# Windowed attention and a feed-forward layer on one core: loads placed a turn earlier, block weights joined by shift-or, largest element by a bfloat16 product, small products grouped

## The chip, the cores and the metric

The kernel runs on one NeuronCore of one Trainium2 chip. The core has five engines, each with its own instruction queue, which it works off in order: TensorE (in profiles PE, its weight loads PEld), VectorE (DVE), ScalarE (ACT), GpSimd (POOL) and SyncE (SP), which here issues transfers. Transfers run on 16 DMA engines. TensorE writes to PSUM, which has eight banks; everything else lives in SBUF. The metric is the device time of the program in microseconds; less is better.

## The reference

Two stages in float32, cut to what matters. The inputs `q`, `k`, `v` are 8 batches x 8 heads x 576 positions x 64; the weights arrive as float64, `w_in` 512 x 2048 and `w_out` 2048 x 512.

```python
scores = scale * np.matmul(q, k.transpose(0, 1, 3, 2))
bias = slopes[:, None, None] * (-np.abs(rel).astype(np.float32))[None, :, :]
mask = (rel >= 0) & (rel < window)               # window = 128
scores = np.where(mask, scores + bias[None], -1000000000.0)
attn = softmax(scores)                            # max, exp, sum, divide
x = matmul(attn, v)  ->  4608 tokens x 512
h = x @ w_in
g = np.where(h >= 1, h, np.where(h <= -1, 0.0, (h + 1) ** 2 / 4))
out = g @ w_out
```

A query sees only the 128 keys up to itself, so a block of 128 queries needs two blocks of keys.

## The kernel before

**Chunks, pairs, turns.** The 4608 tokens are worked in 12 chunks of 384, three blocks of 128. A chunk has eight heads, taken as four pairs; the pairs are numbered p = 0 to 47, four to a chunk, and heads m = 2p and 2p + 1. Chunks 0 and 1 (`LIGHT = 2`) do attention in float32, head by head. From chunk 2 on (p >= 8) attention is done in split float16: a float32 tensor becomes a high and a low half, and a product becomes three products of halves. What the list of steps does for one pair is called a turn here.

**A turn from p = 8 on.** `load_all` (L304, L305, then `load_v`, L376) issues three transfers on SyncE's queue: q, k and v of a later pair. `reach_of` takes the largest absolute values: for v on VectorE (L384), for q and k a sum of absolute values per row on ScalarE (L318). `split_qk` (L367, L368) makes the float16 halves of q and k, `split_v` (L424, L425) those of v. `scores_of_pair` multiplies q and k (L453) and `soften` makes the exponentials: bias and maximum on VectorE (L476), exp on ScalarE (L478). `weights_t` transposes the normalised weights on TensorE (L497), splits them on ScalarE and VectorE (L509, L510) and masks them on GpSimd (L512, L514) into the tile `lu`. `values_of_pair` multiplies `lu` with the halves of v (L557). Once a chunk, `level` (L326 to L335) and `scale_all` (L341 to L358) turn the largest values of the next chunk's four pairs into scales.

**Largest element over partitions.** A column of 128 largest values, one per partition, must become one number in every partition. GpSimd makes a diagonal matrix of the column (L152 in `spread`, L335 in `level`), TensorE multiplies it with a matrix of ones in float32 (L157 in `scale_of`, L341 in `scale_all`), and VectorE takes the maximum of each row. `scale_of` does so 19 times before 175 us, for the weights' blocks, for x of chunks 0 and 1, and for `w_out`; `scale_all` does so ten times, two columns at once.

**Weights.** The float64 weights come in 16 blocks, fetched by `fetch_weights` on ScalarE's queue (`w_in`: L186, `w_out`: L189), each into a tile of its own. `float32_of` makes float32 from the two 32-bit words: two ScalarE instructions in place (L176, L177), then on VectorE a left shift (L178) and an integer sum (L179). `convert_in` and `convert_out` call it, once a block each. All of it happens during chunk 0; the tiles are used for q and k afterwards, with five buffers of one pair each.

**Feed-forward.** For each chunk and each of 16 blocks, `layer1` makes 12 products of 384 columns (L585 to L587), ScalarE, VectorE and GpSimd make g and its halves (L592, L593, L594, L601, L602), and `layer2` makes nine products of 512 columns (L616 to L618), two blocks later. In chunk 0 `layer2` is in float32 (L613).

**What sets the order.** Attention's steps stand in one list, `segments`. While a chunk's feed-forward runs, 32 half-steps a chunk, the next chunk's attention segments are put in between, evenly. A planner then goes through all instructions in this order and puts each on its engine's queue by its own estimate of when it is ready; a later instruction that it takes to be ready may pass an earlier one. `behind(instructions, f)` adds, for what `f` issues, an edge of issue order behind the named instructions. `done_t[m]` names instructions of `weights_t(m)`: from chunk 2 on one of ScalarE, one of VectorE and one of GpSimd, and in the chunks before one of each as well.

The list for the pairs from 8 on, before the change:

```python
if new: segments.append([lambda p=p: reach_of(p + NPAIR)])
segments.append([lambda p=p: scores_of_pair(p, (0, 1))])
if new and g == NPAIR - 1: segments.append([lambda c=c: level(c + 1)])
segments.append([lambda p=p: scores_of_pair(p, (2,))])
segments.append([lambda p=p: split_v(p)])
if p > M1 // 2: segments.append([lambda p=p: values_of_pair(p - 1)])
if new and g == NPAIR - 1: segments.append([lambda c=c: scale_all(c + 1)])
segments.append([lambda p=p: weights_t(2 * p)])
segments.append([split_qk(p + 1)] + [load_all(p + 5)])
segments.append([lambda p=p: weights_t(2 * p + 1)])
```

Of the kernel before, what the change touches and what calls it, by code (L numbers as in the profile page):

```python
# [8 lines left out]
F32 = mybir.dt.float32  # L9
F16 = mybir.dt.float16  # L10
BF16 = mybir.dt.bfloat16
F32R = mybir.dt.float32r
I32 = mybir.dt.int32
U32 = mybir.dt.uint32
# [6 lines left out]
def windowed_attention_then_ffn(  # L21
# [26 lines left out]
    P = 128  # L48
# [56 lines left out]
    for m in range(H):  # L105
# [9 lines left out]
                    compare_op=ALU.is_ge, fill=NEG)  # L115

    sums = const.tile([P, 2, NQB, 2], F32, name="sums")
    G.memset(sums, 1.0e-9)
# [15 lines left out]

    ones = const.tile([P, P], F32, name="ones")
    G.memset(ones, 1.0)
    s_in = const.tile([P, NFC], F32, name="s_in")
# [11 lines left out]
    def spread(name, rows):  # L149

        diag[name] = ap1.tile([P, P], F32, name=f"d_{name}", tag="d", bufs=2)
        G.tensor_scalar(diag[name], ident, rows, None, ALU.mult)  # L152

    def scale_of(name, s, i):

        b = bank(f"m_{name}")[:, :P]
        T.matmul(b, ones, diag.pop(name), start=True, stop=True)  # L157
        top = column(f"top_{name}", "top")
        V.tensor_reduce(top, b, X, ALU.max)
        ti = top.bitcast(I32)  # L160
        V.tensor_scalar(ti, ti, 0x7F800000, None, ALU.bitwise_and)
        V.tensor_scalar(i, top, 2.0 ** -100, 1.0 / TOP, ALU.max, ALU.mult)
        V.reciprocal(s, i)
# [4 lines left out]

    def float32_of(w, name, out=None):

        low, high = w[..., 0], w[..., 1]
        f = stg.tile([P] + list(w.shape[1:-1]), F32, name=f"f_{name}", tag="stg")
        fi = f.bitcast(I32)


        S.activation(high.bitcast(F32), high.bitcast(F32), AF.Prelu, scale=2.0 ** -112, alpha=2.0 ** 32)  # L176
        S.activation(low, low.bitcast(U32), AF.Copy, scale=2.0 ** -29)  # L177
        V.tensor_scalar(fi, high, 3, None, ALU.logical_shift_left)  # L178
        V.tensor_tensor(fi if out is None else out.bitcast(I32), fi, low, ALU.add)  # L179
        return f  # L180

    raw = {}

    def fetch_weights(fc):
        w1 = rawp.tile([P, NCC, P, 2], I32, name=f"rawi{fc}", tag=f"rawi{fc % 3}")
        S.dma_start(w1, wi32[:, 2 * fc * P:2 * (fc + 1) * P].rearrange("(c p) (f w) -> p c f w", p=P, w=2))  # L186

        w2 = rawp.tile([P, DM, 2], I32, name=f"rawo{fc}", tag=f"rawo{fc % 3}")
        S.dma_start(w2, wo32[fc * P:(fc + 1) * P, :].rearrange("p (f w) -> p f w", w=2))  # L189
        raw[fc] = (w1, w2)  # L190

    wide = {}

    def convert_in(fc):
        f = wide[fc] = wp.tile([P, NCC, P], F32, name=f"f_i{fc}", tag="f_i", bufs=3)
        float32_of(raw[fc][0], f"i{fc}", out=f)
        rows = column(f"rows_i{fc}", "rows")
        V.tensor_reduce(rows, f.rearrange("p c f -> p (c f)"), X, ALU.max, apply_absolute_value=True)
        spread(f"i{fc}", rows)
# [8 lines left out]
    def split_in(fc):  # L208
        if fc > 1:
            fall_in(fc)  # L210
        f, s1 = wide.pop(fc), s_in[:, fc:fc + 1]
        t = wi[fc] = wp.tile([P, 2, NCC, P], F16, name=f"wi{fc}", tag=f"wi{fc}")
        S.activation(t[:, 0], f, AF.Copy, scale=s1)
        V.scalar_tensor_tensor(t[:, 1], f, s1, t[:, 0], ALU.mult, ALU.subtract)  # L214
# [4 lines left out]
    def convert_out(fc):  # L219
        wf[fc] = wp.tile([P, DM], F32, name=f"wf{fc}", tag=f"wf{fc}")  # L220
        float32_of(raw[fc][1], f"o{fc}", out=wf[fc])
        S.activation(junk, wf[fc], AF.Abs, accum_out=rows_o[:, fc:fc + 1])
# [58 lines left out]
    def load_qk(p):  # L281
# [9 lines left out]
        for j, r in enumerate(lo_rows):  # L291
            DMA.dma_start(kr[r, j, :n], k[g * P + j * D:g * P + (j + 1) * D, (c + 1) * CH - n:(c + 1) * CH])

    def load_all(p):

        c, g = divmod(p, NPAIR)
        n = CH + before(c) * P
        if c == LIGHT:
            t = wp.tile([P, 2 * CH + P], F32, name=f"qk_{p}", tag=f"wo{NPAIR + g}")
        else:  # L300
            tag = ("rawi0", "rawi1", "rawi2", "rawo0", "rawo1")[p % 5]
            t = rawp.tile([P, 2 * CH + P], F32, name=f"qk_{p}", tag=tag)
        pair[p] = dict(q=t[:, :CH], k=t[:, CH:CH + n])
# [16 lines left out]
    def level(c):  # L320
# [11 lines left out]
        V.tensor_reduce(top[:, 1:2], tops.pop(c)[:, :NPAIR], X, ALU.max)  # L332
        d = diag[c] = ap1.tile([P, 2, P], F32, name=f"d_{c}", tag="qr")
        for a in range(2):
            G.tensor_scalar(d[:, a], ident, top[:, a:a + 1], None, ALU.mult)  # L335
        tops[c, "i"] = iq

    def scale_all(c):

        b = bank(f"m_{c}")[:, :2 * P]  # L340
        T.matmul(b, ones, diag.pop(c).rearrange("p a w -> p (a w)"), start=True, stop=True)  # L341
        i_2[c], s_2[c] = column(f"i_2{c}", "i_2", 3, 2), column(f"s_2{c}", "s_2", 3, 2)
# [9 lines left out]
        V.tensor_scalar(z_of[c], fade, i_2[c][:, 0:1], None, ALU.mult)  # L352
        if "t" not in rels:
            rels["t"] = rawp.tile([P, NQB, 2 * P], F32, name="rels", tag="rawo2")
        rels[c] = rels["t"][:, c % 2], rels["t"][:, 2]
        V.tensor_scalar(rels[c][0], rel, s_2[c][:, 0:1], -1.0e38, ALU.mult, ALU.max)
# [278 lines left out]
    for m in range(M1):  # L635
# [11 lines left out]
        if odd:  # L647
            part["v"] = [[lambda p=p: load_v(p + 4)]] if p < NPAIR else []
            part["v"] += [[lambda x=x: load_all(x)] for x in {5: (8, 9), 6: (10,), 7: (11,)}.get(p, ())]
            part["v"] += [[lambda x=x: reach_of(x)] for x in {3: (4, 5), 4: (6, 7), 6: (8,), 7: (9,)}.get(p, ())]  # L650
# [12 lines left out]
    segments += [[lambda: load_all(p8 + 4)], [lambda: scale_all(LIGHT)], [lambda: split_qk(p8)]]  # L663
    for p in range(M1 // 2, NP):
        c, g = divmod(p, NPAIR)
        new = p + NPAIR < NP
        if new:
            segments.append([lambda p=p: reach_of(p + NPAIR)])
        segments.append([lambda p=p: scores_of_pair(p, (0, 1))])
        if new and g == NPAIR - 1:  # L670
            segments.append([lambda c=c: level(c + 1)])
        segments.append([lambda p=p: scores_of_pair(p, (2,))])
        segments.append([lambda p=p: split_v(p)])
        if p > M1 // 2:
            segments.append([lambda p=p: values_of_pair(p - 1)])
            if g == 0:
                ready.append(len(segments))
        if new and g == NPAIR - 1:
            segments.append([lambda c=c: scale_all(c + 1)])
        segments.append([lambda p=p: weights_t(2 * p)])  # L680
        segments.append(([lambda p=p: split_qk(p + 1)] if p + 1 < NP else []) + ([lambda p=p: load_all(p + 5)] if p + 5 < NP else []))
        segments.append([lambda p=p: weights_t(2 * p + 1)])
    segments.append([lambda: values_of_pair(NP - 1)])
# [127 lines left out]
```

## Time and profile before

| | |
|---|---|
| median of 3 runs | 1027.91 us (1027.88 to 1031.63) |
| profiled execution | 1030.51 us |
| its span, first to last instruction | 1028.3 us |
| TensorE busy | 975.1 us, 95% |
| VectorE, ScalarE, GpSimd busy | 742.2, 618.2, 374.7 us |
| mean granted TensorE clock | 0.979 |
| read from HBM, written | 49.28 MB, 9.44 MB |

Times in the profile are counted from the first instruction. A row of a group gives line, engine, operation, tiles written and read, shapes and count, then busy time and mean length of one, then the engine's idle time just before and what ended it. A row of the list of waits gives who waited for whom: total, times, longest. TensorE's instructions are pipelined and the ends of its matmuls are modelled, so what one costs is read from start to start. Some matmul records can be missing.

### The profile page before, as it was taken

How to read it: one execution, taken by the hardware profiler on the slowest of the kernel's cores; microseconds unless marked ns; L12 is line 12 of the kernel's file. 1: busy time of each engine (PE TensorE's matmuls, PEld its weight loads, DVE VectorE, ACT ScalarE, POOL GpSimd, SP SyncE). 2: the span in 40 equal slices, each digit the busy share in tenths (PEclk: the TensorE clock that was granted, in tenths of full speed). 3: DMA queues.
4: the chain of work that ended last, by engine and by line, in shares of the span. 5: the costliest groups of instructions: out<-in, count | busy, mean ns of one | idle time of the engine just before them, and what ended most of it. 6: DMA issues, size and time to landing. Idle time of an engine off the chain costs nothing.

```text
span 1028.3 us, 17951 instructions
## 1 busy us (share of the span) xinstructions
PE 975.1 (95%) x6218; PEld 548.8 (53%) x6218; DVE 742.2 (72%) x2128; ACT 618.2 (60%) x1547; POOL 374.7 (36%) x479
## 2 busy tenths in 40 slices
PE   7579999997899899899999999999999999999998
PEld 7446554554455455455555555555555555555554
DVE  5789889887767677777777777777777867775322
ACT  4678878665756655655755765765755755654332
POOL 5332211334344323433433433433434434334221
PEclk9889999999799999999999999999999999999999
DMA  8445442002101101201211201111101100000000
GB/s 258 159 154 168 160 142 85 1 11 73 52 22 57 57 24 35 69 30 39 68 40 40 74 24 47 57 30 57 60 29 57 50 2 1 32 1 1 32 1 31
DMA packets 53275, 59.88 MB, mean 58 GB/s; under 512 B 3520, under 2 KB 42432, under 8 KB 53184
## 3 DMA queue, kind: packets, MB, share of 16 engines
q1 hardware_dynamic: 42432, 41.96, 13.0%
q10 hardware_dynamic: 10752, 16.78, 4.8%
q8 instruction: 49, 0.80, 0.3%
q14 instruction: 42, 0.34, 0.1%
HBM read 49.28 MB, written 9.44 MB: 57 GB/s over the span
## 4 chain that ended last, share of the span: by engine, by line
PE 81%; DVE 8%; DMA 4%; ACT 3%; issue 2%; POOL 1%; ACTq 0%; SPq 0%; DVEq 0%; POOLq 0%
PE h L585 11%; PE h L587 11%; PE h L586 11%; PE acc L616 11%; PE acc L617 11%; PE acc L618 11%; PE s L453 5%; PE x L557 4%; PE p L497 3%; DMA vn<-in_v_dram 2%; PE acc L613 2%; PE x L536 1%; DVE g L593 1%; ACT z L478 1%; DVE g L594 1%
## 5 line engine op out<-in xcount | busy, mean ns | idle before, releaser
L602 POOL TENSOR_TENSOR gl<-g,gh 128x384 f16<-128x384 f32 x176 | 164.8, 936 | 394.1 <-ACT gh L601 375.9
L593 DVE SCALAR_TENSOR_TENSOR g<-u,half 128x384 f32<-128x384 f32 x176 | 121.0, 689 | 178.1 <-ACT u L592 167.9
L616 PE MATMUL acc<-wo,gh 128*128 128x512 f16 x528 | 200.0, 380 | 0.4 <-ACT wo L238 0.4
L617 PE MATMUL acc<-wo,gh 128*128 128x512 f16 x528 | 200.3, 379 | 0.0
L618 PE MATMUL acc<-wo,gl 128*128 128x512 f16 x528 | 197.0, 379 | 0.0
L601 ACT CAST gh<-g 128x384 f16<-128x384 f32 x176 | 89.7, 509 | 177.3 <-DVE g L594 124.7
L592 ACT ACTIVATE u<-h,shift,fall 128x384 f32<-128x384 f32 x176 | 116.4, 664 | 88.9 <-PE h L587 88.2
L478 ACT ACTIVATE z<-z,nmax 128x256 f32<-128x256 f32 (+2 forms) x288 | 137.7, 479 | 35.5 <-DVE nmax L476 34.8
L585 PE MATMUL h<-xh,wi 128*128 128x384 f16 x448 | 146.4, 328 | 3.7 <-DVE g L594 3.7
L587 PE MATMUL h<-xh,wi 128*128 128x384 f16 x448 | 147.4, 329 | 1.3 <-DVE wi L214 1.3
L586 PE MATMUL h<-xl,wi 128*128 128x384 f16 x448 | 147.2, 328 | 0.0
L476 DVE CUSTOM_DVE_ANT_0 z<-s,rels,z_of 128x256 f32<-128x256 f32 (+2 forms) x240 | 98.4, 459 | 26.8 <-PE s L453 26.4
L594 DVE SCALAR_TENSOR_TENSOR g<-h,gain,g 128x384 f32<-128x384 f32 x176 | 107.8, 614 | 3.8
L585 PE MATMUL h<-x,wi 128*128 128x384 f16 x320 | 105.3, 331 | 4.4 <-ACT x L566 3.1
L586 PEld LDWEIGHTS <-wi 128*128 128x128 f16 x768 | 75.7, 99 | 62.2 <-issue 9.2
L585 PEld LDWEIGHTS <-wi 128*128 128x128 f16 x768 | 75.5, 98 | 62.1 <-issue 6.6
L586 PE MATMUL h<-x,wi 128*128 128x384 f16 x320 | 105.9, 331 | 0.2 <-DVE x L567 0.2
L587 PE MATMUL h<-x,wi 128*128 128x384 f16 x320 | 105.9, 331 | 0.0
L587 PEld LDWEIGHTS <-wi 128*128 128x128 f16 x768 | 75.7, 99 | 54.6 <-issue 4.2
L512 POOL TENSOR_SCALAR_AFFINE_SELECT lu<-lu 128x768 f16<-128x768 f16 x80 | 72.5, 914 | 71.0 <-DVE lu L510 56.7
L618 PEld LDWEIGHTS <-gl 128*128 128x128 f16 x528 | 51.5, 98 | 58.6 <-issue 1.1
L616 PEld LDWEIGHTS <-gh 128*128 128x128 f16 x528 | 51.6, 98 | 52.0 <-issue 2.2
(154 smaller groups left out, 1555.4 us busy)
## 6 DMA issues: line engine op xcount, KB each, us to landing
out_dram<-o SPq DMA_DIRECT2D x36, 256.0 KB, 2.1
rawi<-in_moe_w_in_dram ACTq DMA_DIRECT2D x16, 512.0 KB, 3.7
rawo<-in_moe_w_out_dram ACTq DMA_DIRECT2D x16, 512.0 KB, 4.7
vn<-in_v_dram SPq DMA_DIRECT2D x32, 256.0 KB, 3.0
qk<-in_q_dram SPq DMA_DIRECT2D x40, 192.0 KB, 3.0
qk<-in_k_dram SPq DMA_DIRECT2D x28, 256.0 KB, 3.5
vn<-in_v_dram SPq DMA_DIRECT2D x16, 192.0 KB, 2.7
qk<-in_k_dram SPq DMA_DIRECT2D x12, 192.0 KB, 2.8
```

The source lines that it names most:

```text
L476: V.tensor_tensor_reduce(out=z[:, i, c0:], in0=pt[:, n, c0:], in1=r[:, c0:], op0=ALU.add, op1=ALU.min, scale=factor, scalar=3.0e38, accum_ ...
L478: S.activation(z[:, i, c0:], z[:, i, c0:], AF.Exp, bias=nmax[:, i:i + 1], scale=-1.0, accum_out=sm[:, i, 0:1])
L585: T.matmul(ph, wi[fc][:, 0, cc, :], xh, start=(cc == 0), stop=False)
L586: T.matmul(ph, wi[fc][:, 0, cc, :], xl, start=False, stop=False)
L587: T.matmul(ph, wi[fc][:, 1, cc, :], xh, start=False, stop=(cc == NCC - 1))
L592: first = S.activation(u, ph, AF.Relu, bias=shift[c] if c else quarter, scale=fall[c][:, col])
L593: V.scalar_tensor_tensor(g, u, half[c] if c else 0.5, u, ALU.min, ALU.mult)
L594: last = V.scalar_tensor_tensor(g, ph, gain[c][:, col] if c else fall[c][:, col], g, ALU.mult, ALU.max)
L602: G.tensor_tensor(gl, g, gh, ALU.subtract)
L616: T.matmul(a, gh[:, ts], wo[fc][:, 0], start=first, stop=False)
L617: T.matmul(a, gh[:, ts], wo[fc][:, 1], start=False, stop=False)
L618: T.matmul(a, gl[:, ts], wo[fc][:, 0], start=False, stop=last)
```

## The change

- **Largest element.** GpSimd's diagonals and the matrix of ones go. The upper 16 bits of each float32 in the column, read as bfloat16, are broadcast to a 128 x 128 stationary operand, and multiplied with a bfloat16 identity: each output row then holds the column. Only the exponent of the result is used. `scale_all` makes two products of 128 columns where one float32 product of 256 stood.
- **Weights.** Both blocks of a step go to one tile, `raw`. ScalarE's two conversions are done once over both; the shift and the sum become one shift-or on VectorE. The low word is scaled by 0.9375 more, so that it stays below the shifted bits.
- **Buffers.** q and k get three tiles for two pairs each in place of five for one each. `rels` moves from one of those tiles to a tile of its own, `near`.
- **Loads.** `load_all(p + 5)` goes to the start of turn p. In the light part `load_v` and `load_all` get `behind(done_t[...])`. In turn 8, `reach_of(12)` moves behind `split_v(8)`.
- **Order in a turn.** `values_of_pair(p - 1)` moves ahead of `scores_of_pair(p, (0, 1))`, in one segment; `split_qk(p + 1)` moves ahead of both `weights_t`, which share a segment.

```diff
-    ones = const.tile([P, P], F32, name="ones")
-    G.memset(ones, 1.0)
+    ident16 = const.tile([P, P], BF16, name="ident16")
+    G.tensor_copy(ident16, ident)
...
-        diag[name] = ap1.tile([P, P], F32, name=f"d_{name}", tag="d", bufs=2)
-        G.tensor_scalar(diag[name], ident, rows, None, ALU.mult)
+        diag[name] = rows
+
+    def across(b, rows):
+
+        r = rows.bitcast(BF16)
+        for a in range(rows.shape[1]):
+            T.matmul(b[:, a * P:(a + 1) * P], r[:, 2 * a + 1:2 * a + 2].broadcast_to([P, P]), ident16, start=True, stop=True)
...
-        T.matmul(b, ones, diag.pop(name), start=True, stop=True)
+        across(b, diag.pop(name))
...
+    def fetch_weights(fc):
+        w = raw[fc] = rawp.tile([P, 2, DM, 2], I32, name=f"raw{fc}", tag=f"raw{fc % 3}")
+        S.dma_start(w[:, 0].rearrange("p (c f) w -> p c f w", c=NCC),
+                    wi32[:, 2 * fc * P:2 * (fc + 1) * P].rearrange("(c p) (f w) -> p c f w", p=P, w=2))
+        S.dma_start(w[:, 1], wo32[fc * P:(fc + 1) * P, :].rearrange("p (f w) -> p f w", w=2))
+
+    def unfold(fc, which=slice(0, 2)):
+
+        low, high = raw[fc][:, which, :, 0], raw[fc][:, which, :, 1]
         S.activation(high.bitcast(F32), high.bitcast(F32), AF.Prelu, scale=2.0 ** -112, alpha=2.0 ** 32)
-        S.activation(low, low.bitcast(U32), AF.Copy, scale=2.0 ** -29)
-        V.tensor_scalar(fi, high, 3, None, ALU.logical_shift_left)
-        V.tensor_tensor(fi if out is None else out.bitcast(I32), fi, low, ALU.add)
-        return f
+        S.activation(low, low.bitcast(U32), AF.Copy, scale=0.9375 * 2.0 ** -29)
+
+    def float32_of(fc, a, out):
+
+        V.scalar_tensor_tensor(out.bitcast(I32), raw[fc][:, a, :, 1], 3, raw[fc][:, a, :, 0], ALU.logical_shift_left, ALU.bitwise_or)
...
     def convert_in(fc):
+        f = wide[fc] = wp.tile([P, DM], F32, name=f"f_i{fc}", tag="f_i", bufs=3)
+        unfold(fc)
+        float32_of(fc, 0, f)
...
-            tag = ("rawi0", "rawi1", "rawi2", "rawo0", "rawo1")[p % 5]
-            t = rawp.tile([P, 2 * CH + P], F32, name=f"qk_{p}", tag=tag)
+            if p % 2 == 0:
+                two[0] = rawp.tile([P, 2, 2 * CH + P], F32, name=f"qk_{p}", tag=f"raw{p // 2 % 3}")
+            t = two[0][:, p % 2]
...
-        d = diag[c] = ap1.tile([P, 2, P], F32, name=f"d_{c}", tag="qr")
-        for a in range(2):
-            G.tensor_scalar(d[:, a], ident, top[:, a:a + 1], None, ALU.mult)
+        diag[c] = top
...
-            part["v"] = [[lambda p=p: load_v(p + 4)]] if p < NPAIR else []
-            part["v"] += [[lambda x=x: load_all(x)] for x in {5: (8, 9), 6: (10,), 7: (11,)}.get(p, ())]
+            part["v"] = [[lambda p=p: behind(done_t[2 * p], lambda: load_v(p + 4))]] if p < NPAIR else []
+            part["v"] += [[lambda p=p, x=x: behind(done_t[2 * p - 1], lambda: load_all(x))] for x in {5: (8, 9), 6: (10,), 7: (11,)}.get(p, ())]
...
-    for p in range(M1 // 2, NP):
+    for p in range(p8, NP):
         c, g = divmod(p, NPAIR)
         new = p + NPAIR < NP
-        if new:
+        if p + 5 < NP:
+            segments.append([lambda p=p: load_all(p + 5)])
+        if new and p > p8:
             segments.append([lambda p=p: reach_of(p + NPAIR)])
-        segments.append([lambda p=p: scores_of_pair(p, (0, 1))])
+        segments.append(([lambda p=p: values_of_pair(p - 1)] if p > p8 else []) + [lambda p=p: scores_of_pair(p, (0, 1))])
+        if p > p8 and g == 0:
+            ready.append(len(segments))
         if new and g == NPAIR - 1:
             segments.append([lambda c=c: level(c + 1)])
         segments.append([lambda p=p: scores_of_pair(p, (2,))])
         segments.append([lambda p=p: split_v(p)])
-        if p > M1 // 2:
-            segments.append([lambda p=p: values_of_pair(p - 1)])
-            if g == 0:
-                ready.append(len(segments))
+        if p == p8:
+            segments.append([lambda p=p: reach_of(p + NPAIR)])
         if new and g == NPAIR - 1:
             segments.append([lambda c=c: scale_all(c + 1)])
-        segments.append([lambda p=p: weights_t(2 * p)])
-        segments.append(([lambda p=p: split_qk(p + 1)] if p + 1 < NP else []) + ([lambda p=p: load_all(p + 5)] if p + 5 < NP else []))
-        segments.append([lambda p=p: weights_t(2 * p + 1)])
+        if p + 1 < NP:
+            segments.append([lambda p=p: split_qk(p + 1)])
+        segments.append([lambda p=p: weights_t(2 * p), lambda p=p: weights_t(2 * p + 1)])
     segments.append([lambda: values_of_pair(NP - 1)])
```

More of the change, by code (lines that the diff above doesn't have):

```diff
@@ L115, in windowed_attention_then_ffn @@
                     compare_op=ALU.is_ge, fill=NEG)
+    near = const.tile([P, 2, 2 * P], F32, name="near")
     sums = const.tile([P, 2, NQB, 2], F32, name="sums")
@@ L167, in windowed_attention_then_ffn @@
     wo32 = w_out.bitcast(I32)
[L169 to L179, printed above, removed]
-        return f
     raw = {}
     def fetch_weights(fc):
[L185 to L190, printed above, removed]
+        w = raw[fc] = rawp.tile([P, 2, DM, 2], I32, name=f"raw{fc}", tag=f"raw{fc % 3}")
[4 more added lines that the diff above has]
+        low, high = raw[fc][:, which, :, 0], raw[fc][:, which, :, 1]
+        S.activation(high.bitcast(F32), high.bitcast(F32), AF.Prelu, scale=2.0 ** -112, alpha=2.0 ** 32)
+        S.activation(low, low.bitcast(U32), AF.Copy, scale=0.9375 * 2.0 ** -29)
+    def float32_of(fc, a, out):
+        V.scalar_tensor_tensor(out.bitcast(I32), raw[fc][:, a, :, 1], 3, raw[fc][:, a, :, 0], ALU.logical_shift_left, ALU.bitwise_or)
     wide = {}
     def convert_in(fc):
-        f = wide[fc] = wp.tile([P, NCC, P], F32, name=f"f_i{fc}", tag="f_i", bufs=3)
-        float32_of(raw[fc][0], f"i{fc}", out=f)
+        f = wide[fc] = wp.tile([P, DM], F32, name=f"f_i{fc}", tag="f_i", bufs=3)
+        unfold(fc)
+        float32_of(fc, 0, f)
         rows = column(f"rows_i{fc}", "rows")
-        V.tensor_reduce(rows, f.rearrange("p c f -> p (c f)"), X, ALU.max, apply_absolute_value=True)
+        V.tensor_reduce(rows, f, X, ALU.max, apply_absolute_value=True)
         spread(f"i{fc}", rows)
@@ L211, in split_in @@
         f, s1 = wide.pop(fc), s_in[:, fc:fc + 1]
-        t = wi[fc] = wp.tile([P, 2, NCC, P], F16, name=f"wi{fc}", tag=f"wi{fc}")
+        t = wp.tile([P, 2, DM], F16, name=f"wi{fc}", tag=f"wi{fc}")
+        wi[fc] = t.rearrange("p s (c f) -> p s c f", c=NCC)
         S.activation(t[:, 0], f, AF.Copy, scale=s1)
@@ L220, in convert_out @@
         wf[fc] = wp.tile([P, DM], F32, name=f"wf{fc}", tag=f"wf{fc}")
-        float32_of(raw[fc][1], f"o{fc}", out=wf[fc])
+        float32_of(fc, 1, wf[fc])
         S.activation(junk, wf[fc], AF.Abs, accum_out=rows_o[:, fc:fc + 1])
@@ L292, in load_qk @@
             DMA.dma_start(kr[r, j, :n], k[g * P + j * D:g * P + (j + 1) * D, (c + 1) * CH - n:(c + 1) * CH])
+    two = [None]
     def load_all(p):
@@ L340, in scale_all @@
         b = bank(f"m_{c}")[:, :2 * P]
-        T.matmul(b, ones, diag.pop(c).rearrange("p a w -> p (a w)"), start=True, stop=True)
+        across(b, diag.pop(c))
         i_2[c], s_2[c] = column(f"i_2{c}", "i_2", 3, 2), column(f"s_2{c}", "s_2", 3, 2)
@@ L352, in scale_all @@
         V.tensor_scalar(z_of[c], fade, i_2[c][:, 0:1], None, ALU.mult)
-        if "t" not in rels:
-            rels["t"] = rawp.tile([P, NQB, 2 * P], F32, name="rels", tag="rawo2")
-        rels[c] = rels["t"][:, c % 2], rels["t"][:, 2]
+        rels[c] = near[:, 0], near[:, 1]
         V.tensor_scalar(rels[c][0], rel, s_2[c][:, 0:1], -1.0e38, ALU.mult, ALU.max)
```

## The prediction

> **What bounds the kernel now.** I read the page first, then the busy time by stretches, then the waits, then the chain of work around the stretches where TensorE stands.
>
> ```profile
> PE 975.1 (95%) x6218; PEld 548.8 (53%) x6218; DVE 742.2 (72%) x2128; ACT 618.2 (60%) x1547; POOL 374.7 (36%) x479
> ```
>
> TensorE is busy for 95% of the span, so only the other 5%, and work taken off TensorE itself, can be won. The stretches say where those 5% lie (columns: stretch, length, then busy us and instruction count of PE, PEld, DVE, ACT, POOL, then granted clock, DMA share, GB/s).
>
> ```profile
> 0.00:80.00 80.00, 55.60 (x288) 42.76 (x289) 57.04 (x204) 47.90 (x130) 33.06 (x72) 0.89 0.60 184
> 80.00:200.00 120.00, 113.74 (x551) 64.94 (x550) 108.81 (x319) 96.85 (x220) 30.76 (x42) 1.00 0.36 119
> 200.00:250.00 50.00, 49.68 (x344) 27.23 (x343) 39.41 (x107) 30.79 (x78) 16.37 (x18) 1.00 0.06 22
> 250.00:300.00 50.00, 39.10 (x266) 21.65 (x266) 36.95 (x111) 30.83 (x87) 20.12 (x22) 0.83 0.19 59
> 300.00:350.00 50.00, 47.10 (x307) 26.01 (x306) 37.77 (x114) 30.41 (x75) 17.74 (x22) 1.00 0.18 59
> 350.00:400.00 50.00, 50.00 (x350) 27.38 (x349) 31.27 (x85) 26.09 (x70) 21.64 (x29) 0.97 0.04 13
> 400.00:500.00 100.00, 96.42 (x653) 52.57 (x654) 75.40 (x222) 62.68 (x162) 36.99 (x42) 0.98 0.16 50
> 500.00:900.00 400.00, 400.00 (x2713) 219.98 (x2713) 299.65 (x853) 243.04 (x626) 160.68 (x194) 1.00 0.13 42
> ```
>
> From 500 us on TensorE never stands: 2713 matmuls in 400 us, 6.78 per us. There the change can win only what it takes off TensorE. From 250 to 500 us there are 266 + 307 + 350 + 653 = 1576 matmuls, worth 232.4 us at that rate, so 17.6 us are lost. From 80 to 200 us TensorE stands 6.3 us, and before 80 us 24.4 us. These are the three pools of time.
>
> What the loss at 250 us is, the chain of waits shows, with TensorE's own order beside it.
>
> ```profile
> 252.98 0.62 DVE h L368
> 253.61 0.34 SPq L304
> 254.00 3.46 DMA qk<-in_k_dram
> 257.54 0.72 ACT junk L318 x2
> ```
> ```profile
> 257.63 0.79 PE L453 MATMUL s<-h 64*128 64x256 f16 x5 [3.38 <-DVE nmax L476]
> 263.55 0.80 PE L585 MATMUL h<-x,wi 128*128 128x384 f16 x2 [3.07 <-ACT x L566]
> 268.85 0.52 PE L586 MATMUL h<-x,wi 128*128 128x384 f16 x1
> 269.17 0.52 PE L587 MATMUL h<-x,wi 128*128 128x384 f16 x1
> ```
>
> `load_all` of a pair waits until `split_qk` (L368) gives its buffer free, and `reach_of` sums the loaded tile (L318) right behind it. ScalarE reaches that sum before the data is there, and the exponentials queued behind it wait too; TensorE then waits 3.38 and 3.07 us for them. Its clock falls: two matmuls of 384 columns start 0.32 us apart here.
>
> The whole list of waits has these:
>
> ```profile
> ACT junk L318 <- DMA qk<-in_q_dram: 43.1, 23, 4.5
> DVE rows L384 <- DMA vn<-in_v_dram: 21.6, 22, 5.6
> PE m_i L157 <- POOL d_i L152: 6.8, 5, 3.2
> PE x L536 <- POOL lu L504: 3.9, 4, 2.1
> PE m_x L157 <- POOL d_x L152: 3.4, 2, 2.1
> ```
>
> Such a wait costs something only where TensorE runs out of other work; from 500 us on it never does.
>
> **The change part by part.** The rows that price it:
>
> ```profile
> L214 DVE SCALAR_TENSOR_TENSOR wi<-f_i,s_in,wi 128x512 f16<-128x512 f32 x16 | 12.4, 773 | 1.6 <-ACT wi L213 1.6
> L179 DVE CUSTOM_DVE_ANT_0 f_i<-rawi,f_i 128x1024 uint16<-128x1024 uint16 x16 | 11.0, 688 | 0.0
> L178 DVE TENSOR_SCALAR f_i<-rawi 128x512 int32<-128x512 int32 x16 | 6.8, 423 | 0.3 <-ACT rawi L176 0.3
> L177 ACT ACTIVATE rawi<-rawi 128x512 int32<-128x512 uint32 x16 | 10.7, 667 | 0.0
> L318 ACT ACTIVATE junk<-qk 128x384 bf16<-128x384 f32 x52 | 27.1, 521 | 43.7 <-DMA qk<-in_q_dram 43.1
> L318 ACT ACTIVATE junk<-qk 128x512 bf16<-128x512 f32 x28 | 17.6, 628 | 3.5 <-DMA qk<-in_k_dram 2.4 <-ACT junk L318 0.4
> L152 POOL TENSOR_SCALAR d_i<-ident,rows_i 128x128 f32<-128x128 f32 x16 | 14.6, 911 | 56.9 <-DVE rc L484 14.9 <-DVE i_in L162 13.0 <-DVE rows_i L198 10.5
> ```
> ```profile
> 629.88 0.59 PE L341 MATMUL m<-d,ones 128*128 128x256 f32 x2
> 630.32 0.33 PE L586 MATMUL h<-x,wi 128*128 128x384 f16 x1
> 630.48 0.33 PE L587 MATMUL h<-x,wi 128*128 128x384 f16 x1
> ```
>
> *Largest element by bfloat16 product, on TensorE.* Two float32 pieces of 256 columns hold TensorE from 629.88 to 630.32, 0.44 us. A 16-bit product of 384 columns takes 0.16 us, so 128 columns take 0.053 us (estimate by proportion). `scale_all` issues two such products where it had the two pieces: 0.44 - 0.11 = 0.33 us, ten times, 3.3 us. `scale_of` had 128 columns, 0.22 us by the same row; with one product 0.17 us are saved, 19 times, 3.2 us. The ten lie where TensorE is full, or nearly, and count whole; the 19 lie before 175 us, where it partly stands. I take **-5**, between -3.3 and -6.5.
>
> *No diagonal on GpSimd.* The wait L157 <- L152 costs TensorE 6.8 + 3.4 = 10.2 us in seven waits. What goes is the GpSimd instruction itself, 0.91 us, so 7 x 0.91 = 6.4 us; what remains late is VectorE's `reduce` ahead of it. I take **-5**, between 0 (the reduce is as late) and -10.2 (all of it).
>
> *One tile for a block's weights, joined by shift-or.* VectorE: 0.423 + 0.688 us become one instruction with two tensor inputs of 512 elements; nearest is L214 with 0.773. That saves 0.34 us a join, 32 joins, 11 us. ScalarE: two of 0.667 us become one of 1024 elements. From 384 to 512 elements L318 grows by 107 ns, so 512 more cost 0.43, and the one takes 1.10 us: 0.24 us saved, 32 times, 7.5 us. All of it lies before 160 us, where VectorE is busy 108.81 of 120 us and is next to the bound. But TensorE stands only 6.3 us in that stretch, and part of that is the wait above. I take **-2**, between 0 and -6.3. Two small risks are inside: `convert_in` now also waits for the block's `w_out`, and a fetch, issued by ScalarE, waits until both joins have let the tile go; the exponentials stand behind it. Both are a block of the loop ahead.
>
> *Loads a turn ahead.* `load_all(p+5)`, three DMAs, moves from behind `split_qk(p+1)` to the start of turn p, and the sums of the pair stay in turn p+1. The buffers go from five to six. At a chunk's first turn the load's buffer was already freed in the turn before, so 254.00's DMA no longer hangs on `scale_all`. On the queue of SyncE it is moved past stores of `out`, which wait for ScalarE's `o`; a load caught behind them now has a turn of some 19 us (below). Of the 17.6 us I take **-12**: two of a chunk's four loads, those of its second tile, still wait for a `split_qk` behind `scale_all`, and the chain of small VectorE steps there stays. Bounds: 0 and -17.6.
>
> By the Trainium skill, TensorE: Matmul & The Clock Gate, section "What's actually happening", the array runs at half clock after an idle window of about 3.4 us until it has been busy for one. The granted clock of 0.83 and the 0.32 us agree. By that rule shortened waits would also return the half-clock matmuls, and this term would lie near its end, -17.6, for 1001 us in all.
>
> *Order edges on the loads.* `behind(done_t[...])` around `load_v` and `load_all` orders issue; `done_t` holds instructions of VectorE, ScalarE and GpSimd, while the loads are issued on SyncE's queue. As I read it an edge of issue order holds on one queue only, so this does nothing: 0.
>
> *Small products grouped.* The six transposes of a pair already run together, and `values_of_pair` already follows scores:
>
> ```profile
> 599.07 0.82 PE L497 MATMUL p<-ident,ep 128*128 128x128 f32 x6
> ...
> 609.92 0.42 PE L453 MATMUL s<-h 64*128 64x192 f16 x5
> 610.27 1.18 PE L557 MATMUL x<-lu,vs 128*64 128x256 f16 x24
> ```
> ```profile
> 602.90 1.99 POOL L512 TENSOR_SCALAR_AFFINE_SELECT lu<-lu 128x768 f16<-128x768 f16 x2
> 604.85 1.67 POOL L514 TENSOR_SCALAR_AFFINE_SELECT lu<-lu 128x768 f16<-128x768 f16 x2
> ```
> ```profile
> L621 ACT ACTIVATE o<-acc,o_g x10: 670/680/692, 508.5 to 738.3; 128x512 f32<-128x512 f32 x10
> ```
>
> So the grouping wins nothing. But it moves `values` nearer to its input. A chunk takes (738.3 - 508.5)/3 = 76.6 us, a turn 19 us. The old list had 34 segments a chunk and `values` five behind the transposes: 5 x 76.6/34 = 11.3 us, and the rows show 610.27 - 599.07 = 11.2. The new list has 30, and `values` three behind: 7.7 us. GpSimd ends its masks at 604.85 + 1.67 = 606.52, 7.45 us after the transposes. The slack falls from 3.75 to 0.2 us. Everything on TensorE stands behind a late `values`. The planner may put it later by itself; I take **+3**, between 0 and the price of the third rival.
>
> Sum: -5 - 5 - 2 - 12 + 3 = **-21**. The profiled execution took 1030.5 us, 2.2 more than its span of 1028.3; its forecast is 1009.5. The median of the runs, 1027.9, lies 2.6 lower, and so does the predicted time: **1007**.
>
> **The rivals.**
>
> *The wait moves to the sums.* `reach_of` has no edge, so the planner may issue it as soon as it thinks the load has landed, with ScalarE waiting as before. For it: 23 waits, so the planner is early nearly always. Against it: a load at a chunk's start no longer hangs on `scale_all`. The loads term falls from -12 to -4: 1015.
>
> The Trainium skill, in the same page's section on the array's architecture, has ScalarE and VectorE as strictly first in, first out; the 257.54 sum ahead of the exponentials agrees.
>
> *`values` waits for GpSimd; slower.* Place: L557, every pair. For it: where the light half of the kernel has `values` close behind the masks, TensorE did wait, 3.9 us in four waits, 0.98 each. Forty pairs at 0.98 are +39 us, with the gains of 24: 1043. It decides above 24/40 = 0.6 us a pair. Against it: in the 400 us from 500 on, nothing on TensorE waits, though the planner set every order there too.
>
> *The early part moves.* If the edges do hold, or the planner puts the loads of later pairs behind the first blocks' weights, this goes:
>
> ```profile
> 22.57 7.44 DMA vn<-in_v_dram
> ```
>
> VectorE stood 5.6 us of it in front of L384. Another -7: 1000.
>
> *Nothing is won.* Loads hidden anyway after 500 us, and the three losses move by a pair rather than go: 1028.
>
> **How the numbers follow.** Forecast 0.42, sums wait 0.17, `values` waits 0.19, early part 0.13, nothing 0.09. Faster by over 0.5%, about what a measurement of this kernel can tell, are the first, second and fourth: 0.72; same 0.09, slower 0.19. The forecast's own range is 990 (the gains at or near their ends: 6.5 + 10.2 + 3 + 17.6) to 1020 (the loads term 0). Taking in half of the slower case, and the early part, the range is 988 to 1038.
>
> **What would show it.** Right: no wait of TensorE over 1 us after 240 us but for the end, granted clock near 1.00 from 250 to 300 us; L157's wait on GpSimd gone; L341's place holding TensorE 0.11 us; ScalarE's wait for `qk` well under 43.1 us. Wrong: TensorE waiting at L557's line on `lu` in many pairs; ScalarE's sums still waiting 3 to 4 us at 250 us; new idle time before 80 us, or a join on VectorE above 0.8 us. The forecast fails if the 17.6 us stay or the waits of `values` pass 0.6 us a pair.

## The result, and the profile after

The changed kernel takes 1138.7 us (median of four runs, 1136.71 to 1139.47) where the kernel before takes 1029.11 beside it. The ratio is 1.1058, with a 95% interval of 1.103 to 1.1087: 110 us slower. The forecast was 1007, and its range ended at 1038.

The page of the changed kernel, its busy line first:

```profile
span 1134.8 us, 17769 instructions
...
PE 1008.8 (89%) x6199; PEld 561.7 (49%) x6199; DVE 736.6 (65%) x2096; ACT 623.6 (55%) x1515; POOL 342.1 (30%) x440
...
PEclk9899999987997996997999899899799899899899
```

The span grew by 106.5 us. TensorE is busy 33.7 us longer (1008.8 against 975.1), though it has 19 matmuls fewer on record, and it stands for 126.0 us where it stood for 53.2: 72.8 us more. The clock line bears on the first part: slices of 0.6 to 0.8 come back about once a chunk (a slice is 28.4 us), and the mean granted clock of the span is 0.938 against 0.979. By stretches (columns as in the prediction), after and then before, with coarser stretches than there:

```profile
0.00:200.00 200.00, 172.26 (x887) 109.09 (x888) 164.58 (x511) 149.55 (x340) 44.86 (x93) 0.97 0.47 148
200.00:500.00 300.00, 266.97 (x1706) 145.45 (x1705) 195.33 (x546) 159.48 (x403) 97.73 (x116) 0.91 0.11 36
500.00:900.00 400.00, 351.28 (x2265) 190.29 (x2264) 260.52 (x752) 215.20 (x550) 126.44 (x148) 0.93 0.13 42
```
```profile
0.00:200.00 200.00, 169.34 (x837) 107.70 (x838) 165.85 (x522) 144.75 (x349) 63.82 (x114) 0.96 0.46 145
200.00:500.00 300.00, 282.31 (x1914) 154.85 (x1913) 220.81 (x634) 180.80 (x470) 112.86 (x132) 0.96 0.13 42
```

Up to 200 us the changed kernel is ahead, 887 matmuls against 837. By the issue times of the `out` stores, the last one of chunk 1 starts at 237.1 us against 248.2, 11.1 us sooner. From there on it falls behind. From 500 to 900 us, where nothing stood before, 2265 matmuls are done in place of 2713. From the last `out` store of chunk 4 to that of chunk 10 a chunk takes 89.4 us, where it took 75.5.

The list of TensorE's waits after, longest first:

```profile
PE x L560 <- POOL lu L517: 30.1, 17, 5.4
PE h L588 <- DVE g L597: 26.2, 8, 5.1
PE p L500 <- DVE ep L492: 20.3, 6, 4.9
```

What stands behind the first of them is seen in TensorE's timeline (start, length, engine, line, operation, tiles, shapes, count; in brackets the wait just before). First the changed kernel:

```profile
518.77 0.82 PE L500 MATMUL p<-ident,ep 128*128 128x128 f32 x6
...
525.47 0.37 PE L560 MATMUL x<-lu,vs 128*64 128x256 f16 x1 [5.01 <-POOL lu L517]
525.77 1.14 PE L456 MATMUL s<-h 64*128 64x128 f16 x12
...
536.08 0.87 PE L500 MATMUL p<-ident,ep 128*128 128x128 f32 x3 [4.68 <-DVE ep L492]
536.75 0.53 PE L588 MATMUL h<-xh,wi 128*128 128x384 f16 x1
537.07 0.53 PE L589 MATMUL h<-xl,wi 128*128 128x384 f16 x1
...
561.37 0.82 PE L500 MATMUL p<-ident,ep 128*128 128x128 f32 x6
...
570.19 0.27 PE L560 MATMUL x<-lu,vs 128*64 128x256 f16 x1
570.39 0.34 PE L456 MATMUL s<-h 64*128 64x128 f16 x5
...
572.24 0.55 PE L456 MATMUL s<-h 64*128 64x128 f16 x7
...
577.74 0.50 PE L456 MATMUL s<-h 64*128 64x256 f16 x5
...
585.27 0.82 PE L500 MATMUL p<-ident,ep 128*128 128x128 f32 x6
```

Then the kernel before:

```profile
599.82 0.28 PE L453 MATMUL s<-h 64*128 64x256 f16 x1
...
604.52 0.82 PE L453 MATMUL s<-h 64*128 64x256 f16 x12
...
617.18 0.49 PE L497 MATMUL p<-ident,ep 128*128 128x128 f32 x3
```

Scores of a pair are 12 products for the first two blocks and six for the third. Before, one of the 12 goes 0.75 us behind the transposes (599.07 to 599.82); the other 11 begin 5.4 us behind (604.52), and the third block's last five 10.8 us behind (609.92, in the prediction's rows). After, all 12 stand behind the first product of `values`, which waits for its masked weights: they begin 7.0 us behind the transposes at 525.77; in the next turn but one five go 9.0 us behind at 570.39 and seven from 572.24 on, and the third block's last five 16.4 us behind (577.74). From transposes to transposes this turn takes 23.9 us (561.37 to 585.27), the one shown of the kernel before 18.1 (599.07 to 617.18); a quarter of the mean chunk is 22.4 against 18.9.

The feed-forward's own products fill some of that. At a chunk's end they run out: TensorE stands 5.01 and 4.68 us within 18 us, and behind the second stop matmuls of 384 columns start 0.32 us apart. The chain of waits (start, length, what) leads from the masks by way of `values` and the scores to the weights that the second stop waits for:

```profile
524.60 0.83 POOL lu L517
...
525.47 0.37 PE x L560
525.84 1.09 PE s L456 x12
...
527.35 1.88 ACT z L481 x8
...
530.79 2.79 DMA vn<-in_v_dram
...
535.47 0.48 DVE ep L492
```

A late v has a small part in it: VectorE waits 1.07 and 0.55 us for v (L387) ahead of the halves that are masked for the first stop, and 0.17 us ahead of `ep`. At 704.5 us, with 0.26 us of such waiting, the first stop is still 3.5 us.

Three small things came as foretold. The bfloat16 products hold TensorE from 510.11 to 510.24, 0.13 us in place of 0.44, and TensorE's wait in `scale_of` is down from 10.2 to 0.7 us. The joins on VectorE take 687 and 763 ns. TensorE's timeline of the changed kernel, and then its groups of instructions by shape, have the rows:

```profile
510.11 0.28 PE L159 MATMUL m<-ident,tt 128*128 128x128 bf16 x2
510.24 0.33 PE L590 MATMUL h<-x,wi 128*128 128x384 f16 x1
```
```profile
L192 DVE SCALAR_TENSOR_TENSOR wf<-raw 128x512 int32<-128x512 int32 x16 | 12.2, 763 | 0.0
L192 DVE SCALAR_TENSOR_TENSOR f_i<-raw 128x512 int32<-128x512 int32 x16 | 11.0, 687 | 1.0 <-ACT raw L188 0.6
...
L159 PE MATMUL m_i<-ident,rows_i 128*128 128x128 bf16 x16 | 3.6, 226 | 0.7 <-DVE rows_i L201 0.7
```

### The profile page after: what moved, and what is told of

It reads as the page before. It is cut to its first block, busy times and chain, and to the rows that moved or that the text cites. A ratio compares the mean times of both kernels' runs of the same rounds, so it can differ in the third digit from the quotient of the medians.

```text
span 1134.8 us, 17769 instructions
## 1 busy us (share of the span) xinstructions
PE 1008.8 (89%) x6199; PEld 561.7 (49%) x6199; DVE 736.6 (65%) x2096; ACT 623.6 (55%) x1515; POOL 342.1 (30%) x440
## 4 chain that ended last, share of the span: by engine, by line
PE 65%; DVE 14%; DMA 8%; ACT 7%; issue 3%; POOL 2%; SPq 1%; ACTq 0%; DVEq 0%; POOLq 0%
PE h L588 10%; PE h L589 9%; PE h L590 9%; PE acc L619 8%; PE acc L620 8%; PE acc L621 8%; PE s L456 4%; DMA vn<-in_v_dram 4%; PE x L560 3%; DMA qk<-in_k_dram 2%; PE p L500 2%; ACT z L481 2%; DVE h L371 2%; DVE g L596 2%; PE acc L616 1%
## 5 line engine op out<-in xcount | busy, mean ns | idle before, releaser
L605 POOL TENSOR_TENSOR gl<-g,gh 128x384 f16<-128x384 f32 x176 | 168.4, 958 | 525.6 <-ACT gh L604 477.9
L596 DVE SCALAR_TENSOR_TENSOR g<-u,half 128x384 f32<-128x384 f32 x176 | 115.8, 658 | 220.0 <-ACT u L595 202.3
L588 PE MATMUL h<-xh,wi 128*128 128x384 f16 x448 | 150.3, 338 | 20.2 <-DVE g L597 12.4
L589 PE MATMUL h<-xl,wi 128*128 128x384 f16 x448 | 151.6, 338 | 1.7 <-DVE xl L582 1.5
L590 PE MATMUL h<-xh,wi 128*128 128x384 f16 x448 | 151.6, 338 | 1.1 <-DVE wi L218 0.8
L479 DVE CUSTOM_DVE_ANT_0 z<-s,near,z_of 128x256 f32<-128x256 f32 (+2 forms) x240 | 98.3, 459 | 46.6 <-PE s L456 46.5
L588 PE MATMUL h<-x,wi 128*128 128x384 f16 x320 | 108.2, 342 | 17.9 <-DVE g L597 13.8
L589 PEld LDWEIGHTS <-wi 128*128 128x128 f16 x768 | 77.5, 101 | 89.2 <-issue 38.7
L588 PEld LDWEIGHTS <-wi 128*128 128x128 f16 x768 | 76.8, 100 | 74.9 <-issue 22.2
L589 PE MATMUL h<-x,wi 128*128 128x384 f16 x320 | 109.4, 342 | 0.1
L590 PE MATMUL h<-x,wi 128*128 128x384 f16 x320 | 109.3, 342 | 0.0
L590 PEld LDWEIGHTS <-wi 128*128 128x128 f16 x768 | 77.7, 101 | 59.9 <-issue 12.6
L515 POOL TENSOR_SCALAR_AFFINE_SELECT lu<-lu 128x768 f16<-128x768 f16 x80 | 69.7, 879 | 97.3 <-DVE lu L513 83.5
L560 PE MATMUL x<-lu,vs 128*64 128x256 f16 (+1 forms) x888 | 62.3, 269 | 30.9 <-POOL lu L517 30.1
```

The source lines that it names most:

```text
L479: V.tensor_tensor_reduce(out=z[:, i, c0:], in0=pt[:, n, c0:], in1=r[:, c0:], op0=ALU.add, op1=ALU.min, scale=factor, scalar=3.0e38, accum_ ...
L588: T.matmul(ph, wi[fc][:, 0, cc, :], xh, start=(cc == 0), stop=False)
L589: T.matmul(ph, wi[fc][:, 0, cc, :], xl, start=False, stop=False)
L590: T.matmul(ph, wi[fc][:, 1, cc, :], xh, start=False, stop=(cc == NCC - 1))
L596: V.scalar_tensor_tensor(g, u, half[c] if c else 0.5, u, ALU.min, ALU.mult)
L605: G.tensor_tensor(gl, g, gh, ALU.subtract)
```

## The experiments

Ratios are against the kernel before on the same chip, with a 95% interval; chunk lengths are the mean over chunks 5 to 10, from one last `out` store to the next. Line numbers of profiles are those of the kernel shown.

### Is it the order of the turn?

**The kernel before with the new order of the turn alone.** Products, weights and buffers stay old, and `load_all` stays beside `split_qk`.

```diff
-        segments.append([lambda p=p: scores_of_pair(p, (0, 1))])
+        segments.append(([lambda p=p: values_of_pair(p - 1)] if p > p8 else []) + [lambda p=p: scores_of_pair(p, (0, 1))])
...
-        if p > M1 // 2:
-            segments.append([lambda p=p: values_of_pair(p - 1)])
...
-        segments.append([lambda p=p: weights_t(2 * p)])
         segments.append(([lambda p=p: split_qk(p + 1)] if p + 1 < NP else []) + ([lambda p=p: load_all(p + 5)] if p + 5 < NP else []))
-        segments.append([lambda p=p: weights_t(2 * p + 1)])
+        segments.append([lambda p=p: weights_t(2 * p), lambda p=p: weights_t(2 * p + 1)])
```

> The kernel before with the new order of a turn alone: values of the pair before ahead of the scores, split_qk ahead of both weights_t, loads where they were. Theory O (values ahead of the scores puts GpSimd's masks into the loop from one turn to the next, so a turn takes 23 us where the feed-forward gives it 19) and rival G (the grouping of both weights_t at the end of the turn delays the first head) both expect 1110 to 1150 us, with TensorE waiting some 10 us at every chunk's end. Rival L (the loads, the new buffers or the other parts do it) expects 1020 to 1035.

Measured: 1137.96 us, ratio 1.1064 [1.1038, 1.109]. The order of the turn alone does all the harm; none of the other edits is needed for it.

**The changed kernel with the whole old order of the turn.** Loads ahead, buffers, products and shift-or stay new.

```diff
-        segments.append(([lambda p=p: values_of_pair(p - 1)] if p > p8 else []) + [lambda p=p: scores_of_pair(p, (0, 1))])
+        segments.append([lambda p=p: scores_of_pair(p, (0, 1))])
...
+        if p > p8:
+            segments.append([lambda p=p: values_of_pair(p - 1)])
...
+        segments.append([lambda p=p: weights_t(2 * p)])
         if p + 1 < NP:
             segments.append([lambda p=p: split_qk(p + 1)])
-        segments.append([lambda p=p: weights_t(2 * p), lambda p=p: weights_t(2 * p + 1)])
+        segments.append([lambda p=p: weights_t(2 * p + 1)])
```

> The changed kernel with the whole order of a turn undone (values behind split_v, the two weights_t apart with split_qk between them); loads ahead, six buffers, bfloat16 products and shift-or stay. If grouping the transposes is worth nothing, as the prediction had it, this is the 1020.06 us of the run with values late, within 4 us. The prediction's terms for the other parts (-5, -5, -2, -12) make it 1003 to 1007.

Measured: 1019.24 us, ratio 0.9916 [0.9884, 0.9948], chunk 75.4 us. It beats both kernels. All the other edits together are worth 10 us, not 24.

### Which part of the order?

**`values_of_pair` back behind `split_v`,** in a segment of its own; the transposes stay together.

```diff
-        segments.append(([lambda p=p: values_of_pair(p - 1)] if p > p8 else []) + [lambda p=p: scores_of_pair(p, (0, 1))])
+        segments.append([lambda p=p: scores_of_pair(p, (0, 1))])
...
         segments.append([lambda p=p: split_v(p)])
+        if p > p8:
+            segments.append([lambda p=p: values_of_pair(p - 1)])
```

> The changed kernel with values_of_pair back in a segment of its own behind split_v, five segments behind the transposes; split_qk and the grouped weights_t stay new. O expects 1000 to 1030 us and turns of 18 to 19 us from 500 us on. G expects 1100 or more, as does L.

Measured: 1020.06 us, ratio 0.9918 [0.989, 0.9946]. That is within 1 us of the kernel with the whole old turn.

**The transposes apart again,** `values` left where the change put it.

```diff
+        segments.append([lambda p=p: weights_t(2 * p)])
         if p + 1 < NP:
             segments.append([lambda p=p: split_qk(p + 1)])
-        segments.append([lambda p=p: weights_t(2 * p), lambda p=p: weights_t(2 * p + 1)])
+        segments.append([lambda p=p: weights_t(2 * p + 1)])
```

> The changed kernel with the two weights_t in segments of their own again, split_qk between them; values stay ahead of the scores. G expects 1000 to 1060 us; O and L expect 1120 to 1150, with TensorE still waiting at each chunk's end.

Measured: 1136.88 us, ratio 1.1057 [1.1023, 1.1091]. Grouping the transposes neither costs nor wins anything that can be told from nothing; it is the place of `values` that counts.

**Scores first, `values` second, in the same segment.** This tells apart whether `values` is too near its masks, or whether it is what stands behind `values` that suffers: the distance to the masks stays that of the change.

```diff
-        segments.append(([lambda p=p: values_of_pair(p - 1)] if p > p8 else []) + [lambda p=p: scores_of_pair(p, (0, 1))])
+        segments.append([lambda p=p: scores_of_pair(p, (0, 1))] + ([lambda p=p: values_of_pair(p - 1)] if p > p8 else []))
```

> The changed kernel with scores_of_pair(p, (0, 1)) ahead of values_of_pair(p - 1) inside their shared segment, nothing else moved. If O holds by the order of the two alone (scores behind values), 1000 to 1060 us; if it is the distance from the transposes (three segments in place of five) that decides, the turn's length stays and 1100 or more is measured. G and L expect 1130 or so.

Measured: 1038.65 us, ratio 1.0101 [1.0078, 1.0123], chunk 78.8 us. TensorE's timeline with scores first:

```profile
521.84 0.82 PE L500 MATMUL p<-ident,ep 128*128 128x128 f32 x6
522.59 0.23 PE L456 MATMUL s<-h 64*128 64x128 f16 x1
...
527.61 0.67 PE L456 MATMUL s<-h 64*128 64x128 f16 x11
...
528.21 0.30 PE L560 MATMUL x<-lu,vs 128*64 128x256 f16 x1
...
540.41 0.82 PE L500 MATMUL p<-ident,ep 128*128 128x128 f32 x6
```

Of the 119 us between the changed kernel and the one with `values` late, 100 hang on the order of two calls in one segment. One product of scores again goes 0.75 us behind the transposes, the other 11 begin 5.8 us behind (527.61), and this turn is 18.6 us. The other 19 us are what the nearness of `values` to the masks costs, or its place in the planner's list; no run tells these two apart. TensorE's own waits for `lu` come to 3.0 us in that kernel.

### Why do scores stand behind `values`?

Both take their PSUM bank from one pool of three (`ps_a`): the transposes of a pair use two, `scores_of_pair(p, (0, 1))` two, `values` one. So when the transposes are issued one bank is free. My theory: banks are given out in the list's order, so with `values` first the free bank goes to it, and lies there until the masks are done; with scores first, they start in it at once. If so, the order must cease to matter when `values` has a bank of its own. The rival, an order that the planner takes from the list whatever the banks, would leave the gap.

**The changed kernel with a bank of its own for `values`.** PSUM has eight banks, and the other five are taken, so the shared pool shrinks to two.

```diff
-    ps_a = ctx.enter_context(tc.tile_pool(name="ps_a", bufs=3, space=PSUM))
+    ps_a = ctx.enter_context(tc.tile_pool(name="ps_a", bufs=2, space=PSUM))
+    ps_x = ctx.enter_context(tc.tile_pool(name="ps_x", bufs=1, space=PSUM))
...
-        px = bank(f"x_{p}")[:, :CH]
+        px = ps_x.tile([P, 4 * P], F32, name=f"x_{p}", tag="ps_x")[:, :CH]
```

> The changed kernel with its turn order untouched (values ahead of the scores), but the tile of values_of_pair takes a PSUM bank of its own, and scores, transposes and the small products share two banks in place of three. Theory B (the three banks are handed out in program order, so the scores queue for a bank behind values, which cannot start before GpSimd's masks are done; the new order does its harm through the bank) expects that the scores start right behind the transposes again and that most of the 110 us go: 1030 to 1070 us, some of it lost to having two banks. Rival I (the order of the instructions does the harm, whatever the bank) expects 1110 or more.

Measured: 1081.51 us, ratio 1.0518 [1.0491, 1.0545]: 57 us of the loss go, and the time lies between what the two theories expected.

**The same banks, with scores first in the segment** (both edits above).

> The same two banks and one, with the scores ahead of values in the shared segment. B expects the same time as the run with values ahead, within 10 us, since neither can hold up the other's bank. I expects it 80 us or more below that run, as with three banks (1038.65 against 1138.7).

Measured: 1085.57 us, ratio 1.0554 [1.0535, 1.0574]. With a bank of its own for `values`, the order of the two calls moves the time by 4 us, the other way round and with intervals that overlap; with the shared pool it moved it by 100. So here the order does its harm only where `values` shares the scores' pool. How it does so is my reading, and no run measured it: neither by which rule the planner hands out banks, nor whether it is the bank itself that the scores lack or their place behind `values` on TensorE's queue. And the test is not a clean one: with two shared banks, neither order lets scores start at once. In the timeline of the first of the two, scores now go ahead of `values`, though the list still has `values` first:

```profile
565.53 0.82 PE L501 MATMUL p<-ident,ep 128*128 128x128 f32 x6
...
570.71 0.23 PE L457 MATMUL s<-h 64*128 64x128 f16 x1
...
571.19 0.67 PE L457 MATMUL s<-h 64*128 64x128 f16 x11
...
572.11 0.30 PE L561 MATMUL x<-lu,vs 128*64 128x256 f16 x1
```

It also shows the price of two banks, which I had put too low: both are full of transposes, and the first product of scores begins 5.2 us behind them (565.53 to 570.71). With scores first, three banks took 1038.65 us and two and one 1085.57: 47 us for the third bank.

### What are the other parts worth?

**Old turn and old places of the loads,** on the changed kernel: the experiment with the old turn, with `load_all(p + 5)` back beside `split_qk(p + 1)` and `reach_of(12)` back in its place.

```diff
-        if p + 5 < NP:
-            segments.append([lambda p=p: load_all(p + 5)])
...
-        if p == p8:
-            segments.append([lambda p=p: reach_of(p + NPAIR)])
...
-        if p + 1 < NP:
-            segments.append([lambda p=p: split_qk(p + 1)])
+        segments.append(([lambda p=p: split_qk(p + 1)] if p + 1 < NP else []) + ([lambda p=p: load_all(p + 5)] if p + 5 < NP else []))
```

> As the run with the old turn, with load_all(p + 5) back beside split_qk(p + 1) and reach_of(12) back at the head of its turn; six buffers, products and shift-or stay. By the prediction the loads are worth 12 us: this is 8 to 15 us above the run with the old turn. If the stop at 250 us has another cause, the two are equal within 4 us.

Measured: 1021.11 us, ratio 0.9934 [0.9908, 0.996]. The loads' new place is worth 1.9 us of the 12 foretold, by the two medians, and their intervals overlap. With the loads ahead, the stop is still there, sooner: the stretches of the kernel with the old turn and early loads, and its chain of waits (start, length, what) at the stop.

```profile
200.00:250.00 50.00, 43.10 (x304) 23.70 (x303) 39.28 (x111) 27.69 (x68) 19.78 (x20) 0.96 0.15 48
250.00:300.00 50.00, 46.32 (x312) 25.74 (x309) 33.85 (x95) 31.20 (x85) 19.93 (x22) 0.91 0.11 33
```
```profile
244.53 1.66 DVE h L371 x2
...
246.22 2.44 DMA qk<-in_q_dram
...
248.68 0.03 ACT junk L325
```

The two stretches hold 616 matmuls, where the kernel before did 610. The load that ScalarE waits for still starts as `split_qk` (L371) lets its tile go, 0.03 us after its end at 246.19. It is the load of the next chunk's third pair, the first of its second tile.

**Weights and buffers alone:** the kernel before with one tile for a block's weights, shift-or, six buffers and `near`; the order edges on the light part's loads are in it too.

```diff
-        V.tensor_scalar(fi, high, 3, None, ALU.logical_shift_left)
-        V.tensor_tensor(fi if out is None else out.bitcast(I32), fi, low, ALU.add)
+        V.scalar_tensor_tensor(out.bitcast(I32), raw[fc][:, a, :, 1], 3, raw[fc][:, a, :, 0], ALU.logical_shift_left, ALU.bitwise_or)
```

> The kernel before with a block's weights in one tile, ScalarE's conversions over both and the shift-or, and the six buffers and the tile near that go with them; order, loads and float32 products as before. The prediction's term is -2: 1023 to 1029 us; lower if VectorE's 11 us before 160 us were on the path.

Measured: 1028.32 us, ratio 0.9986 [0.9968, 1.0004]. It is not told from nothing, as its term (-2) allowed.

**Products alone:** the kernel before with `across` in `scale_of` and `scale_all`, and no diagonals.

```diff
-        G.tensor_scalar(diag[name], ident, rows, None, ALU.mult)
+        diag[name] = rows
...
-        T.matmul(b, ones, diag.pop(c).rearrange("p a w -> p (a w)"), start=True, stop=True)
+        across(b, diag.pop(c))
```

> The kernel before with the bfloat16 products and without GpSimd's diagonals, nothing else. The prediction's two terms, -5 and -5, make it 1015 to 1022 us. If the waits they end are taken up by the next stop, it is 1024 to 1029.

Measured: 1041.17 us, ratio 1.0116 [1.0088, 1.0145]: slower, against every theory I had set down. Its chunk is 79.4 us. Two runs look for the reason.

**Products alone with a sixth buffer:**

```diff
-            tag = ("rawi0", "rawi1", "rawi2", "rawo0", "rawo1")[p % 5]
+            tag = ("rawi0", "rawi1", "rawi2", "rawo0", "rawo1", "rawo2")[p % 6]
...
-        rels[c] = rels["t"][:, c % 2], rels["t"][:, 2]
+        rels[c] = near[:, 0], near[:, 1]
```

> The kernel before with the bfloat16 products, and a sixth q and k buffer, with `rels` in a tile of its own; weights and list of steps stay as before. The products alone took 1041 us, with a chunk of 79.4 us where the kernel before has 75.5, and with q and k late at the chunk's boundary. If the loads are late because a buffer comes free too late (theory A), the sixth buffer brings the chunk back to about 75.5 us and the time to 1018 to 1028. If the products alone make the planner put another order on TensorE, whatever the buffers (theory B), the chunk stays near 79 us and the time at 1036 to 1044.

Measured: 1046.01 us, ratio 1.016 [1.013, 1.019]. Theory A is out: the buffer is not what is lacking. The time is 2 us above what theory B expected.

**Products in `scale_of` only;** `scale_all` keeps diagonals and the float32 product.

```diff
-        across(b, diag.pop(c))
+        T.matmul(b, ones, diag.pop(c).rearrange("p a w -> p (a w)"), start=True, stop=True)
```

> The kernel before with the bfloat16 products in `scale_of` alone (the 19 before 175 us); `scale_all` keeps GpSimd's diagonals and the float32 product of 256 columns. If what makes the products alone slow lies in `scale_all`, once a chunk (theory B, and also theory A), the chunk is back at 75.5 us and what is left is the gain of the early part: 1020 to 1028. If the 19 early products shift the whole order after them, the chunk stays near 79 us and the time is 1035 to 1044.

Measured: 1026.65 us, ratio 0.9974 [0.9959, 0.9988]. So the 19 early products win some 3 us, and the loss comes with what is done once a chunk: the products of `scale_all` and the diagonals that go with them. Where it arises, the chain of waits of the kernel with products and six buffers shows, at one chunk's end:

```profile
579.83 4.27 DMA qk<-in_k_dram
...
584.61 0.19 ACT junk L325
584.79 1.15 ACT o L624 x2
585.94 0.57 ACT u L595
...
587.79 0.54 DVE g L597
...
588.37 0.48 PE h L588
```

ScalarE's queue has the sum over a late k (L325) ahead of the `o` and `u` that the feed-forward needs, and TensorE stands. In the kernel with old turn and old loads, which has the same products, ScalarE does `u`, `gh` and `o` first at that place and no such wait appears there. Why the planner sets the sum ahead in the one and behind in the other stays open.

## Why the prediction was wrong

**The step that failed** is "Small products grouped", with its sentence "Everything on TensorE stands behind a late `values`. The planner may put it later by itself; I take +3, between 0 and the price of the third rival." It measured about +119: 1138.7 less the 1019.24 of the same kernel with the old turn. I found the place (L560), the wait (`lu`), and that the slack would vanish. But I asked only whether `values` would be late, and priced the lateness as a wait of TensorE: 0.98 us a pair. Nor do the six transposes of a pair always run together in the kernel before, as I read from one turn: at 617.18 only three do. The wait itself is 30.1 us in 17 waits, less than that rival's 39. What I did not ask is what stands behind `values` while it waits: the next pair's scores. Where in the turns shown one of their products began 0.75 us behind the transposes and the others 5.4, they now begin 7 to 9 us behind or later, and with them the chain of bias, exponentials and transposes starts later: a turn takes 22.4 us on average in place of 18.9. At the chunk's end TensorE has no other work to cover that. The stop of 536.08, for `ep`, is on that chain; that the others in the list after (26.2 us for `g`, 20.3 for `ep` in all) are its too is argued from this one. That `values` holds up the scores by way of the one free bank is the reading above, which the runs with a bank of its own agree with and do not prove.

**Rival "`values` waits for GpSimd; slower"** (0.19) had the sign and the place; its 1043 was 96 us short, for the same reason. My argument against it, that from 500 us on nothing on TensorE waits, was no argument: in the old order a pair's scores went ahead of `values`.

**Half clock.** Behind the stop that ends at 536.08, matmuls of 384 columns follow each other after 0.32 us, where 0.16 us is the pace of the prediction's rows at 630.32; that pace is how TensorE can be busy 33.7 us longer with fewer matmuls. The rule of the Trainium skill (TensorE: Matmul & The Clock Gate, "What's actually happening") of half clock behind an idle window agrees with that; here it worked against the change.

**Loads a turn ahead,** -12: measured -2. The mechanism was named ("two of a chunk's four loads, those of its second tile, still wait for a `split_qk` behind `scale_all`") and mis-sized: those two are the ones the stop at 248 us hangs on. My test for it failed too: in the list of waits of the kernel with the old turn and early loads, ScalarE still waits 41.1 us for `qk` (43.1 before). As far as the loads go, this is the rival in which the sums wait. The rival of the early part did not come by its way: VectorE waits 24.4 us for `vn` after, 21.6 before, and the transfer that was to go, 7.44 us at 22.57, is there with 7.43 us at 22.84. Yet the early part did gain: the last `out` store of chunk 0 starts at 166.5 us after, at 173.3 before. Which edit wins that stays open.

```profile
ACT junk L325 <- DMA qk<-in_q_dram: 41.1, 22, 4.9
```

**Products, no diagonal, shift-or:** -5, -5 and -2. Together, with old turn and old loads, they gave -8 by the medians, -6.8 by the ratio of 0.9934; the early products alone -3, the weights no more than -3.3 by their interval. As prices of instructions they were right: 0.13 us against 0.11 foretold for two products, 1154 and 1139 ns against 1.10 us for ScalarE's double conversions, 687 and 763 ns against 773 on VectorE. What was wrong is to add them as if the order stood still. The products of `scale_all` with their missing diagonals, a gain of 3.3 us by the sum for the products, turned the early products' -3 into +12 when nothing else was changed.

**Order edges on the loads,** 0: the run of weights and buffers has them too and is not told from nothing; no run has them alone.

**What would show it:** of the signs that I named, the clock from 250 to 300 us should have been near 1.00; in the changed kernel it is 0.82. Of the signs of being wrong, the waits at L557's line on `lu` came.

## What to carry to other kernels

When a step is moved up in a list, ask not only when its inputs are ready, but what stands behind it while it waits, on its engine's queue and for a buffer of a shared pool. With three banks and five wanted, try the order that puts first the step that can start at once; here the exchange of two calls in a line is worth 100 us of 1139. And measure small savings in the kernel they are for: one that frees 0.3 us of TensorE a chunk went with another order that costs 4.

## What the runs showed that I had not expected

One bank of PSUM, shared or set apart, is worth 47 us here (1038.65 with three shared, 1085.57 with two and one), where all the other edits together gain 10. A wait of 30.1 us in the list stands for a loss of 119: most of it lies in what began later, not in the wait. And the bfloat16 products once a chunk, cheaper on TensorE (0.13 us against 0.44), made the kernel 1.2% slower alone, 1.6% with a sixth buffer, and were in the version that is 0.8% faster.
